# Linear attention on one core: half of the 17th head's output rows stored by GpSimd's queue

## The chip, the core and the metric

One NeuronCore of a Trainium2 chip runs one program on its five engines: TensorE (PE), VectorE (DVE), ScalarE (ACT), GpSimd (POOL) and SyncE (SP). Sixteen DMA engines move data between DRAM and the on-chip memory SBUF. The metric is the device time of one execution in microseconds (us), as a median over runs.

## The reference

Linear attention for 32 heads, each with 2048 rows of 128 bf16 elements in `q`, `k` and `v`:

```python
phi_q = jnp.where(q > 0, q + 1, jnp.exp(q)) + 1e-6
phi_k = jnp.where(k > 0, k + 1, jnp.exp(k)) + 1e-6
kv = jnp.einsum("bhsd,bhse->bhde", phi_k, v)
z = jnp.einsum("bhsd->bhd", phi_k)
num = jnp.einsum("bhqd,bhde->bhqe", phi_q, kv)
den = jnp.einsum("bhqd,bhd->bhq", phi_q, z)[..., None] + 1e-6
return num / den
```

Each head reads 1.5 MB and writes 0.5 MB: 50.33 MB read and 16.78 MB written in all.

## The kernel before

A head's 2048 rows lie in SBUF as 128 partitions of 16 rows each, so one partition is 16 x 128 bf16 = 4 KB, contiguous in DRAM. Each operation of head `h` has a key with a part number, such as `ldk16.0`, and the program runs each engine through a list of keys written out by hand (`ORDER`). An operation names the operations that it depends on, and the program turns these into semaphore waits.

For each head `h`:

- `ldq`, `ldk`, `ldv` (line 340) load 512 KB each, into rings of 7 buffers (`NI`).
- `ek` (ScalarE, line 366) and `em` (VectorE, 344) make min(exp(k), 1) + 1e-6; `rk` (GpSimd, 351; VectorE for the first heads) makes max(k, 0). The sum of the two is phi_k.
- `v1` (GpSimd, 376) copies `v` beside a column of ones, so that one product gives both kv and z.
- `kv` (TensorE, 383) sums 32 products of 128 x 129; `kvs` (VectorE, 355) takes the sum to SBUF.
- `T` (TensorE, 393) transposes `q`; `eq` (ScalarE, 397), `emq` (VectorE, 344), `rqa` (ScalarE, 349) and `rqb` (VectorE, 350) do for `q` what was done for `k`.
- `n` (TensorE, 415, 420, 422) makes numerator and denominator in two parts; `a` (435), `r` (438) and `f` (442), on VectorE, divide, and write the result into one of 16 output buffers (`NO`).
- `st` (line 450) stores the head's output, 512 KB, from SBUF to DRAM.

All loads but one (`ldv0.0`, on ScalarE's queue) and all stores are issued by SyncE, in the order of its list: loads first, and stores more and more towards the end, the 17th head's `st16.0` after `st17.0` and before `st14.0`. With 16 output buffers nothing waits for `st16.0` but the end of the program. After its last store SyncE waits for the semaphore of every output buffer (line 468).

A DMA of 128 partitions puts 8 partitions on each of the sixteen DMA engines, as descriptors of 4 KB. Two stores are cut by partitions: head 12 into 51, 64 and 13 (`ROWS`), and the first half of the columns of head 14 into 68 and 60 (`HALF`). `st_parts(h)` gives the parts of a head as columns a:b and partitions x:y.

GpSimd's list holds only `rk` and `v1` of the heads, and two operations of the start that make the identity matrix. In the middle of the kernel it reads `rk20.0 rk21.0 v121.0 rk22.0 v122.0 v123.0 rk23.0`. `rk22.0` waits for `kv20`, as there are two buffers for each of `rk` and `v1`.

Of the kernel before, what the change touches and what calls it, by code (L numbers as in the profile page):

```python
# [13 lines left out]
NI, NO, NE, NR, NV, NQ, NK = 7, 16, 2, 2, 2, 2, 2  # L14
# [31 lines left out]
def na(h):  # L46
    return NA[h] if h else 0


def groups(h):  # L50
    if h == NH - 1:
        return ((0, 2, 3, 0), (6, 2, 3, 2), (12, 2, 2, 4))
    return ((0, 4, 3, 0), (12, 2, 2, 4))


HALF = {14: ((0, 68), (68, 128))}
ROWS = {12: ((0, 51), (51, 115), (115, 128))}


def st_parts(h):  # L60
    tiles = ((0, 6), (6, 12), (12, 16)) if h == NH - 1 else WHOLE
    if h in HALF:
        tiles = HALVES
    return tuple((a, b, x, y) for i, (a, b) in enumerate(tiles)
                 for x, y in (HALF.get(h, ()) if i == 0 and h in HALF else ROWS.get(h, ((0, P),))))

# [20 lines left out]
def rqb_parts(h):  # L87
# [4 lines left out]
    if h == NH - 1:  # L92
# [48 lines left out]
    "POOL": """  # L141
        ident0 ident v10.0 rk4.0 v14.0 rk5.0 v15.0 rk6.0 v16.0 rk7.0 v17.0 v18.0 rk8.0 rk9.0 v19.0 rk10.0
        v110.0 v111.0 rk11.0 v112.0 rk12.0 v113.0 rk13.0 v114.0 rk14.0 v115.0 rk15.0 v116.0 rk16.0 rk17.0
        v117.0 rk18.0 v118.0 v119.0 rk19.0 v120.0 rk20.0 rk21.0 v121.0 rk22.0 v122.0 v123.0 rk23.0 v124.0
        rk24.0 rk25.0 v125.0 rk26.0 v126.0 rk27.0 v127.0 rk28.0 v128.0 rk29.0 v129.0 rk30.0 v130.0 rk31.0
        v131.0
    """,
# [25 lines left out]
class Program:  # L173
# [10 lines left out]
    def add(self, eng, key, fn, deps=(), dma=None, inc=True):  # L184
        assert key not in self.op, key
        self.op[key] = (eng, fn, tuple(deps), dma, inc)
# [71 lines left out]
def bass_standalone__linear_attn_elu__prompt_kernel(nc: bass.Bass, q: bass.AP, k: bass.AP, v: bass.AP, out: bass.AP):  # L258
    B, H, S, D = q.shape
    assert D == P and S == 16 * P and B * H == NH  # L260
    NT = S // P
# [5 lines left out]
    qf, kf, vf, of = (t.rearrange("b h s d -> (b h) s d") for t in (q, k, v, out))  # L267
    rows = lambda t, h: t[h].rearrange("(p j) d -> p j d", j=NT)

    with ExitStack() as es:  # L270
# [17 lines left out]
        o_sb = sb([P, NO, NT, D])  # L288
# [7 lines left out]
        pr = Program(sem)  # L296
        add = pr.add
# [59 lines left out]
        def head(h):  # L357
# [15 lines left out]
            for i, (a, b) in enumerate(v_parts(h)):  # L373
                key = f"v1{h}.{i}"
# [25 lines left out]
            n = na(h)  # L400
# [46 lines left out]
                                [[m, nb], [1, m], [0, D]]), op=ALU.mult)  # L447
                add("DVE", f"f{h}.{i}", g, [f"r{h}.{i}"] + freed(NO, h, ("st", st_parts)))
            for i, (a, b, x, y) in enumerate(st_parts(h)):
                add("SP", f"st{h}.{i}", lambda e, a=a, b=b, x=x, y=y: e.dma_start(  # L450
                    rows(of, h)[x:y, a:b], o_sb[x:y, h % NO, a:b]),
                    [f"f{h}.{j}" for j, (t0, nb, m, b0) in enumerate(groups(h)) if t0 < b and a < t0 + nb * m],
                    dma=f"o{h % NO}")

        for h in range(NH):
            head(h)
# [7 lines left out]
        for e, engine in (("POOL", nc.gpsimd), ("SP", nc.sync), ("ACT", nc.scalar), ("PE", nc.tensor), ("DVE", nc.vector)):  # L464
            pr.emit(e, engine)
        last = f"o{(NH - 1) % NO}"
        for name in [f"o{s}" for s in range(NO) if f"o{s}" in pr.count and f"o{s}" != last] + [last]:
            nc.sync.wait_ge(pr.get(name), pr.count[name])


# [26 lines left out]
```

## Time and profile before

| | |
|---|---|
| time, median of 3 runs | 169.11 us (169.07 to 169.39) |
| the profiled execution | 169.41 us, span 168.1 us |
| granted TensorE clock in it | 0.988 |
| mean DMA rate over the span | 402 GB/s |
| stores on SyncE's queue | 38, of which 29 of 512 KB |
| a 512 KB store, issue to landing | 14.0 us median |

Times of single operations count from the start of the span. The span is the time between the first and the last instruction of the program in the profile; the profiled execution's own time is 1.3 us longer. Matmuls are pipelined, so a busy TensorE is not one at its peak. The DMA table lists queues: q1 is SyncE's, q10 ScalarE's, and q8 and q14 fetch instructions. A DMA's landing is the time at which its semaphore is full. "Issue" is the time that the issuing engine's sequencer spends on it; the data moves later.

### The profile page before, as it was taken

Reading aid. Unit: us, or ns where it says so; the run is one execution under the profiler, and the core shown is the slowest. Engines: PE = TensorE matmul, PEld = TensorE weight load, DVE = VectorE, ACT = ScalarE, POOL = GpSimd, SP = SyncE. Lnnn points to the kernel's source line nnn. Section 1 sums busy time; section 2 is a strip of 40 time slices with the busy share of each in tenths; the row PEclk is TensorE's granted clock in tenths of the full one; section 3 lists DMA queues with packets and bytes.
Section 4 is the critical chain, followed back from the end, with each engine's and each line's share of the span. In section 5 each row is a group of like instructions: output and inputs, shape, how many; then the busy total and the mean of one; then the engine's idle time right before and its main releaser. Section 6 shows DMA issues by size and latency. Waiting matters only on the chain.

```text
span 168.1 us, 6169 instructions
## 1 busy us (share of the span) xinstructions
PE 155.7 (93%) x2709; PEld 150.8 (90%) x2709; DVE 155.8 (93%) x309; ACT 149.4 (89%) x101; POOL 84.4 (50%) x63
## 2 busy tenths in 40 slices
PE   3999999999999999999599999999999999999650
PEld 1689999999999999999589999999999999999640
DVE  0499999999999999999999999999999999999971
ACT  3799999999999999999669999999999999997600
POOL 1100355566666666546926667676555566670000
PEclk9999999999999999999999999999999999999995
DMA  5999999999999999999999999999999999999996
GB/s 212 409 420 414 401 407 411 401 409 406 407 409 403 408 411 417 407 406 416 406 421 414 418 412 408 421 412 416 414 415 416 414 417 411 415 415 414 375 406 243
DMA packets 18910, 67.51 MB, mean 402 GB/s; under 512 B 2115, under 2 KB 2499, under 8 KB 18883
## 3 DMA queue, kind: packets, MB, share of 16 engines
q1 hardware_dynamic: 18739, 66.59, 98.6%
q8 instruction: 21, 0.34, 0.8%
q10 hardware_dynamic: 144, 0.52, 0.8%
q14 instruction: 6, 0.05, 0.1%
HBM read 50.33 MB, written 16.78 MB: 399 GB/s over the span
## 4 chain that ended last, share of the span: by engine, by line
DVE 52%; PE 40%; DMA 2%; ACT 2%; issue 1%; SPq 0%
DVE la L442 24%; PE la L383 16%; DVE la L344 14%; PE la L420 9%; PE la L422 8%; PE la L393 7%; DVE la L350 7%; DVE la L438 3%; DMA la<-in_k_dram 2%; DVE la L355 2%; ACT la L397 1%; DVE la L376 1%; DVE la L435 1%; ACT la L366 1%; PE la L415 0%
## 5 line engine op out<-in xcount | busy, mean ns | idle before, releaser
L442 DVE TENSOR_TENSOR la<-la 128x1536 bf16<-128x1536 f32 (+2 forms) x65 | 78.0, 1200 | 0.6
L351 POOL TENSOR_SCALAR la<-la 128x2048 bf16<-128x2048 bf16 x28 | 54.1, 1935 | 38.2 <-PE la L383 38.2
L420 PE MATMUL la<-la 128*128 128x129 bf16 x512 | 67.0, 219 | 0.3 <-DVE la L355 0.3
L422 PE MATMUL la<-la 128*128 128x129 bf16 x512 | 67.0, 219 | 0.0
L397 ACT ACTIVATE la<-la 128x2048 bf16<-128x2048 bf16 (+2 forms) x35 | 60.3, 1729 | 5.9 <-PE la L422 2.9
L366 ACT ACTIVATE la<-la 128x2048 bf16<-128x2048 bf16 (+1 forms) x33 | 61.4, 1860 | 3.3 <-DMA la<-in_k_dram 3.2
L383 PE MATMUL la<-la 128*128 128x129 bf16 x1024 | 63.4, 220 | 0.0
L383 PEld LDWEIGHTS la<-la 128*128 128x128 bf16 x1024 | 59.4, 98 | 0.7 <-DVE la L355 0.5
L422 PEld LDWEIGHTS la<-la 128*128 128x128 bf16 x512 | 49.6, 97 | 0.0
L420 PEld LDWEIGHTS la<-la 128*128 128x128 bf16 x512 | 47.9, 97 | 0.5 <-DVE la L355 0.4
L344 DVE TENSOR_SCALAR la<-la 128x2048 bf16<-128x2048 bf16 (+2 forms) x68 | 44.9, 697 | 0.0
L376 POOL COPY la<-la 128x1024 int32<-128x1024 int32 (+1 forms) x29 | 30.7, 1058 | 26.9 <-PE la L383 16.6
L393 PE MATMUL la<-la 128*128 128x128 bf16 x512 | 35.6, 222 | 2.2 <-DMA la<-in_q_dram 1.1
L393 PEld LDWEIGHTS la<-la 128*128 128x128 bf16 x512 | 30.8, 99 | 3.5 <-DMA la<-in_q_dram 2.0
L349 ACT ACTIVATE la<-la 128x1024 bf16<-128x1024 bf16 (+2 forms) x31 | 33.1, 1067 | 0.0
L350 DVE TENSOR_SCALAR la<-la 128x1024 bf16<-128x1024 bf16 (+2 forms) x37 | 23.7, 646 | 5.7 <-DMA la<-in_k_dram 4.3
L415 PE MATMUL la<-la 128*128 128x3 bf16 (+1 forms) x128 | 21.6, 168 | 2.7 <-DVE la L442 1.7
L415 PEld LDWEIGHTS la<-la 128*128 128x128 bf16 x128 | 12.5, 98 | 3.2 <-DVE la L442 2.1
L438 DVE RECIPROCAL la<-la 128x12 f32<-128x12 f32 (+2 forms) x65 | 12.8, 199 | 1.4 <-PE la L422 0.8
L355 DVE CAST la<-la 128x129 bf16<-128x129 f32 x32 | 8.0, 251 | 0.0
L331 PE MATMUL la<-la 128*128 128x480 bf16 x21 | 6.3, 441 | 1.5 <-POOL la L316 1.5
L331 PEld LDWEIGHTS la<-la 128*128 128x128 bf16 x21 | 2.2, 114 | 3.5 <-POOL la L316 1.5
(15 smaller groups left out, 10.3 us busy)
## 6 DMA issues: line engine op xcount, KB each, us to landing
la<-in_q_dram SPq DMA_DIRECT2D x32, 512.0 KB, 14.8
la<-in_k_dram SPq DMA_DIRECT2D x32, 512.0 KB, 14.8
la<-in_v_dram SPq DMA_DIRECT2D x31, 512.0 KB, 14.5
out_dram<-la SPq DMA_DIRECT2D x29, 512.0 KB, 14.0
la<-in_v_dram ACTq DMA_DIRECT2D x1, 512.0 KB, 5.8
out_dram<-la SPq DMA_DIRECT2D x2, 256.0 KB
out_dram<-la SPq DMA_DIRECT2D x2, 192.0 KB, 3.1
out_dram<-la SPq DMA_DIRECT2D x1, 204.0 KB
```

The source lines that it names most:

```text
L344: add(on(key, "DVE"), key, lambda e: e.tensor_scalar(t, t, 1.0, EPS, op0=ALU.min, op1=ALU.add), deps)
L349: "ACT": lambda e: e.activation(dst, src, ACT.Relu),
L350: "DVE": lambda e: e.tensor_scalar(dst, src, 0.0, None, op0=ALU.max),
L351: "POOL": lambda e: e.tensor_scalar(dst, src, BIG, 0.0, op0=ALU.min, op1=ALU.max)}[eng], deps)
L366: add("ACT", f"ek{h}.{i}", lambda e, a=a, b=b: e.activation(em_sb[:, h % NE, a:b], k_sb[:, h % NI, a:b], ACT.Exp), over("ldk", h, ldk_part ...
L383: ins = e.matmul(kv_ps, lhsT=src[:, j], rhs=v1_sb[:, h % NV, j, 0:NC], start=(j + part == 0), stop=(j == NT - 1 and part == 1))
L393: ins = e.transpose(xT[:, j], q_sb[:, h % NI, j], ident[:])
L397: add("ACT", f"eq{h}.{i}", lambda e, a=a, b=b: e.activation(emq_sb[:, h % NQ, a:b], xT[:, a:b], ACT.Exp), over("T", h, t_parts, a, b) + fr ...
L415: e.matmul(_ap(o_ps[:, :], o + D, [[NC, m]]), lhsT=ones[:], rhs=epsr[:, 0:m], start=True, stop=False, skip_group_check=True)
L420: e.matmul(to, lhsT=emq_sb[:, h % NQ, t], rhs=kvs_sb[:, h % NK, 0:NC], start=late and c == 0, stop=False, skip_group_check=True)
L422: ins = e.matmul(to, lhsT=rq_sb[:, h % NQ, t], rhs=kvs_sb[:, h % NK, 0:NC], start=False, stop=True, skip_group_check=True)
L442: return e.tensor_tensor(out=_ap(o_sb[:, :, :, :], first(o_sb[:, h % NO, t0, 0:1]) - first(o_sb[:, :, :, :]), [[m * D, nb], [D, m], [1, D] ...
```

## The change

`st16` is cut into three parts by partitions: 0 to 63 stay with SyncE, at the same place of its list (`st16.0`). Partitions 64 to 95 (`st16.1`) and 96 to 127 (`st16.2`) are issued by GpSimd, `st16.1` between `v121.0` and `rk22.0`, `st16.2` between `v122.0` and `v123.0`. In DRAM the 32 partitions of a part lie one behind the other, 128 KB; for `st16.1` that destination is written as 2 runs of 64 KB, for `st16.2` as 4 runs of 32 KB. The source stays 32 partitions of 4 KB. Each part has its own semaphore (`p16.1`, `p16.2`), and SyncE waits for these two first in its closing waits.

```diff
-ROWS = {12: ((0, 51), (51, 115), (115, 128))}
+ROWS = {12: ((0, 51), (51, 115), (115, 128)), 16: ((0, 64), (64, 96), (96, 128))}
+BY_POOL = {"st16.1": 2, "st16.2": 4}
...
-        v117.0 rk18.0 v118.0 v119.0 rk19.0 v120.0 rk20.0 rk21.0 v121.0 rk22.0 v122.0 v123.0 rk23.0 v124.0
+        v117.0 rk18.0 v118.0 v119.0 rk19.0 v120.0 rk20.0 rk21.0 v121.0 st16.1 rk22.0 v122.0 st16.2 v123.0 rk23.0 v124.0
...
-                add("SP", f"st{h}.{i}", lambda e, a=a, b=b, x=x, y=y: e.dma_start(
-                    rows(of, h)[x:y, a:b], o_sb[x:y, h % NO, a:b]),
+                key = f"st{h}.{i}"
+                to = rows(of, h)[x:y, a:b]
+                if key in BY_POOL:
+                    to = of[h, NT * x:NT * y].rearrange("(g r) d -> g (r d)", g=BY_POOL[key])
+                add("POOL" if key in BY_POOL else "SP", key, lambda e, a=a, b=b, x=x, y=y, to=to: e.dma_start(
+                    to, o_sb[x:y, h % NO, a:b]),
...
-                    dma=f"o{h % NO}")
+                    dma=f"p{h}.{i}" if key in BY_POOL else f"o{h % NO}")
...
-        for name in [f"o{s}" for s in range(NO) if f"o{s}" in pr.count and f"o{s}" != last] + [last]:
+        for name in [n for n in pr.count if n[0] == "p"] + [f"o{s}" for s in range(NO) if f"o{s}" in pr.count and f"o{s}" != last] + [last]:
```

## The prediction, on record before the result

> **What bounds the kernel now.** I read the page first, then the stretches, the waits and chain of the end, and last the packets and completion events of single DMAs.
>
> ```profile
> PE 155.7 (93%) x2709; PEld 150.8 (90%) x2709; DVE 155.8 (93%) x309; ACT 149.4 (89%) x101; POOL 84.4 (50%) x63
> DMA  5999999999999999999999999999999999999996
> q1 hardware_dynamic: 18739, 66.59, 98.6%
> q8 instruction: 21, 0.34, 0.8%
> q14 instruction: 6, 0.05, 0.1%
> ```
>
> TensorE, VectorE and the 16 DMA engines are all full; GpSimd is half idle. So the question is which of them ends last. The table of stretches, and the waits of SyncE's queue after 150 us:
>
> ```profile
> core 0: us, PE busy (x) PEld busy (x) DVE busy (x) ACT busy (x) POOL busy (x), PEclk, DMA share, GB/s
> 140.00:150.00 10.00, 10.00 (x186) 10.00 (x184) 9.93 (x19) 9.91 (x7) 6.69 (x5) 1.00 1.03 415
> 156.00:160.00 4.00, 2.38 (x45) 2.20 (x42) 3.93 (x11) 2.85 (x3) 0.00 (x0) 1.00 0.93 373
> 164.00:168.10 4.10, 0.00 (x0) 0.00 (x0) 0.70 (x1) 0.00 (x0) 0.00 (x0) 0.53 0.63 240
> ```
> ```profile
> SPq L450 <- DVE la L344: 5.8, 1, 5.8
> SPq L468 <- DMA out_dram<-la: 2.4, 2, 1.3
> ```
> ```profile
> 163.74 0.96 DVE la L442
> ```
>
> The last line is the last piece of the chain: VectorE ends at 164.70 and the last store (st31.1) is issued at 164.72. The span ends at 168.10, after SyncE's waits at L468 for stores. So the last 3.4 us are stores only, and the DMA share there is 0.63: some engines are done and others not. The trace keeps sixteen completion events per full DMA, one for each engine. For st24.0 they run 156.62, 156.72, 156.96, then 159.60, 159.64, 159.72, 159.98, then nine from 160.59 to 161.78. Behind it stand st29, st19, st28, st30 (512 KB each) and st31 in three pieces. On the latest engine the queue never empties: st30.0 reaches it at 166.72, st31 takes 1.33 us more, 168.05, and the last event is at 168.06. The three earliest engines run dry and wait for issues. What a last store needs without a queue: st31.0, issued 163.64, has its first event at 165.36, 1.72 us; st31.1 so would be home near 164.72 + 1.7 + 0.2 for the spread = 166.6. The end is thus set by the latest DMA engine, 1.4 us behind compute, not by the sum of bytes. A change of who carries the rows counts fully there.
>
> Why they differ: a 16 KB instruction packet (21 on q8, 1.05 us each) sits on one engine at a time. After that at 16.46 one engine's event of ldk4.0 falls from 18.0 to 19.4, and it keeps the lag. SP's partial stores are already uneven the other way. st12.0 (51 rows) has three data events (88.85, 88.91, 90.08), st14.0 (68 half rows) four (152.47, 153.11, 153.72, 154.25). Followed from DMA to DMA, the three engines of st12.0 are among the four of st14.0, so SP's narrow stores begin with the same engines; and one of those three, call it x, is the one that ends last (154.25, 155.49 at st21.0, 161.78 at st24.0). At st16.0 the four stand at 151.12, 151.73, 152.34 and 152.89 (x): 1.77, 1.16 and 0.55 us ahead of x.
>
> **The price of a row.** A 4 KB packet has a median of 159 ns, and an engine steps 1.25 us from one 512 KB DMA (8 rows each) to the next: 0.157 us a row, the same for loads and stores.
>
> **The change, part by part.** st16.0 on SP keeps 64 of 128 rows: 4 instead of 8 rows for each engine, -4 x 0.157 = -0.63 us on all sixteen. st12.1, also 64 rows, shows that this is spread over sixteen (sixteen events). The 32 + 32 rows come back on GpSimd's queue. On SP, 51 rows used 3 engines, 13 used 13, 60 used 15 and 68 used 4: the largest divisor up to 16. With 2 and 4 runs on the DRAM side I take 2 and 4 engines: 16 rows each on two engines, 8 each on four. Net: two engines +12 rows, +1.88 us; four engines +4 rows, +0.63 us; the rest -0.63 us.
>
> Which engines, no row shows, as GpSimd issues no data DMA before. Bounds: at best the two and the four are all early ones and the end moves by -0.63 us; at worst both stores start with the same first engines as SP's narrow ones, 16 + 8 + 4 - 8 = +20 rows, +3.1 us. The nearest row is SP's own narrow store, which starts with x's group. If x is one of the two: +1.88 us. If x is in the group but only among the four: x moves +0.63, but the engine 0.55 us ahead of it, carrying 16 rows, ends at -0.55 + 1.88 = +1.33 us. Were the two instead among the other late engines (up to 161.48 at st24.0), the end would move about -0.3 + 1.88 = +1.6 us. I take +1.7 us, between 1.33 and 1.88.
>
> The Trainium skill, "DMA: Bandwidth & Descriptors", section "Why a DMA increments its semaphore by 16 and not by 1", says that a DMA uses as many engines as divide the slowest dimension on both sides, SyncE's on the lowest-numbered, GpSimd's on consecutive ones from a moving cursor. By it, with a cursor at zero, the sum is +1.33 or +1.88 us and not +3.1, as the second store does not fall on the first's engines; the trace agrees on SyncE's half (3, 13, 15, 4).
>
> GpSimd's side. st16.1 needs f16.0 and f16.1 (ended 98.12), long done when its turn comes behind v121.0:
>
> ```profile
> 102.97 1.03 POOL L376 COPY la<-la 128x1024 int32<-128x1024 int32 x1
> 105.67 1.96 POOL L351 TENSOR_SCALAR la<-la 128x2048 bf16<-128x2048 bf16 x1 [1.67 <-PE la L383]
> 107.57 1.03 POOL L376 COPY la<-la 128x1024 int32<-128x1024 int32 x1
> 110.26 1.11 POOL L376 COPY la<-la 128x1024 int32<-128x1024 int32 x1 [1.66 <-PE la L383]
> ```
>
> It falls into the 1.67 us that GpSimd waits for kv20, ahead of rk22.0; st16.2 into the 1.66 us behind v122.0, ahead of v123.0. Behind them queue rk22.0 and v122.0 (end 108.60) for kv22, which starts at 113.00, and v123.0 and rk23.0 (end 113.23) for kv23 at 117.62: 4.4 us spare each. What one issue costs GpSimd no row shows: SP's issues take 0.33 to 2.39 us, ScalarE's one 0.41. Even 2.39 leaves 0.7 us outside the wait and inside the 4.4: nothing. Without that cover, past some 6 us each, kv22 and all behind it would slip.
>
> Loads. From 104 us to st16.0's turn (its events began at 149.14) the two engines run 16 rows, 2.5 us, later, and SP's loads behind them too. Least room between the last event of a load and its first use after 104 us: 3.2 us (ldk24, ldq24 and ldv27), 3.4 for ldv31. 2.5 fits, so compute should keep its 164.70; the 24 rows of the worst case, 3.8 us, would not quite. SP's closing waits grow by two semaphores that are long full: about 0.07 us each at 165 us, ahead of the wait that ends at 168.06, so nothing.
>
> Sum: 0 on compute, +1.7 us on the last engine. The profiled execution took 169.41 us with a span of 168.10, 1.3 us outside it; the median of the three times is 169.11. Span 168.1 + 1.7 = 169.8; 169.11 + 1.7 = 170.8 us for the median.
>
> **Rivals.** *The rows fall on early engines.* Three engines have 5.2 us to spare at st24.0 and three more 2.1 to 2.2; if the two carry 16 rows there and the four are early or middling, x loses 4 rows: -0.63 us, 168.5 us. If the four include one of the late ones at 161.2 to 161.5, it gains 0.63 and the end stands between 0 and +0.35. For it: there is real idle time there, and x is one engine. Against it: the two must be neighbours out of six or seven of sixteen, and nothing but a start away from SP's first engines would bring them there. It decides at 1.9 us: an engine that stands less than that ahead of x ends later than x does now if it carries 12 rows more.
>
> *The split is even after all.* If GpSimd's stores spread 2 rows over each of the sixteen, every engine has its 8 again and only the order changes: 169.1 us. For it: the source has 32 rows, divisible by 16. Against it: the two-run destination, and the events of 51 and 68 rows. The Trainium skill's "DMA: Bandwidth & Descriptors", section "Rules for kernel authors", holds that spreading DMAs over SP, ACT and GpSimd saves issue time only, as all run on the same engines; by that it would be 169.1 too. The 5.2 us between first and last engine here is what speaks against it.
>
> *GpSimd's descriptor work holds up VectorE.* VectorE is busy 19.86 of 20 us from 100 to 120, so each microsecond lost there moves 164.70; but compute has 1.4 us before it reaches the DMA end. Alone it decides only past 1.4 us; 2 us of it would give 169.1 + 0.6 = 169.7 us.
>
> **How the numbers follow.** The heavy pair on late engines, 0.59, +1.3 to +1.9 us (170.4 to 171.0) and a tail to +3.1, and the stall of VectorE, 0.03: slower, 0.62. Rows on early engines, 0.25, 168.5 to 168.9: faster. Even split, or the pair early and one of the four late, 0.13: within 0.2%, 168.8 to 169.4, which is about what a measurement here can tell from no change. The range 168.5 to 171.2 takes in the faster case and the slower one, and leaves out the two stores on the same engines (172.2), less than 1 in 10, and a stall of compute on top.
>
> **What would show it.** Right: a GpSimd queue in the DMA table with 64 packets of 4 KB; some engines' events of st24.0 moving by +1.9 and +0.6 us and the others by -0.6; VectorE still ending near 164.7; SyncE's closing wait for stores longer than 2.4 us. Wrong: last events earlier by 0.6 (the pair was early), all unchanged (even split), VectorE's end later than 166 (a stall), or waits of kv22 on GpSimd.

## The result: 0.6% slower, and the times spread

| | before | after |
|---|---|---|
| median, same chip | 169.26 us (169.07 to 169.88, 18 runs) | 170.18 us (169.33 to 171.02, 18 runs) |
| the profiled execution | 169.41 us, span 168.1 us | 169.33 us, span 168.0 us |

The ratio is 1.0056, with a 95% interval of 1.0037 to 1.0074: 0.95 us (0.63 to 1.25). The times of before lie within 0.8 us, those of after are strewn over 1.7 us. The profiled execution of after is the earliest of its 18, no slower than before. It shows what the change did, but not the loss; the loss shows in late executions, those that took longer, which the experiments gave.

The page of after, the lines that answer to those of before:

```profile
PE 156.6 (93%) x2709; PEld 151.4 (90%) x2709; DVE 155.7 (93%) x309; ACT 149.4 (89%) x101; POOL 85.3 (51%) x65
DMA  5999999999999999999999999999999999999996
q1 hardware_dynamic: 18675, 66.33, 98.2%
q8 instruction: 21, 0.34, 0.8%
q0 software_dynamic: 96, 0.26, 0.4%
out_dram<-la POOLq DMA_DIRECT2D x2, 128.0 KB, 5.5
```

GpSimd has two instructions more. q0 is its queue: 64 packets of 4 KB for data and 32 small ones for the semaphores, sixteen for each DMA. SyncE's q1 has exactly 64 packets fewer. Landing took 5.5 us from the issue.

GpSimd's timeline in the middle of the kernel (start, length, instruction, in brackets the idle time before it):

```profile
103.97 0.66 POOL L455 DMA_DIRECT2D out_dram<-la  x1
105.71 1.94 POOL L352 TENSOR_SCALAR la<-la 128x2048 bf16<-128x2048 bf16 x1 [1.08 <-PE la L384]
107.60 1.03 POOL L377 COPY la<-la 128x1024 int32<-128x1024 int32 x1
108.58 0.54 POOL L455 DMA_DIRECT2D out_dram<-la  x1
110.29 1.10 POOL L377 COPY la<-la 128x1024 int32<-128x1024 int32 x1 [1.17 <-PE la L384]
```

An issue takes 0.66 and 0.54 us, and each lies inside the wait: the idle time of 1.67 us before has become 1.08 us, and rk22.0 starts at 105.71 us after 105.67. The rows themselves went out as follows: of the 32 packets of st16.1 all sixteen engines took two each, side by side, all started between 107.79 and 108.37 us, with sixteen completion events from 108.75 to 109.14; of st16.2 as well, from 112.46 to 113.06 us, with one engine late at 113.42 and 113.73. Two runs in DRAM or four made no difference: the split is even.

The table of stretches (length, busy time of each engine, granted clock, DMA share, GB/s), SyncE's closing wait, and the last line of the chain:

```profile
140.00:150.00 10.00, 10.00 (x185) 10.00 (x183) 9.93 (x19) 9.91 (x7) 6.69 (x6) 1.00 1.03 415
156.00:160.00 4.00, 2.41 (x45) 2.23 (x42) 3.93 (x11) 2.85 (x3) 0.00 (x0) 1.00 0.93 375
164.00:168.00 4.00, 0.00 (x0) 0.00 (x0) 1.00 (x2) 0.00 (x0) 0.00 (x0) 0.50 0.64 246
```
```profile
SPq L473 <- DMA out_dram<-la: 1.8, 2, 1.3
```
```profile
164.08 0.96 DVE la L443
```

Everything is as before: compute ends at 165.04 us (164.70 before; the granted clock from 160 to 165 us is 0.68 here and 0.92 there), the same tail of stores follows, and st24.0's last event is at 161.67 us after 161.78. No engine moved by +1.9, +0.6 or -0.6 us.

### The profile page after: what moved, and what is told of

Read it like the earlier page. It is cut to its first block, busy times and chain, and to the rows that moved or that the text cites. A ratio compares the mean times of both kernels' runs of the same rounds, so it can differ in the third digit from the quotient of the medians.

```text
span 168.0 us, 6172 instructions
## 1 busy us (share of the span) xinstructions
PE 156.6 (93%) x2709; PEld 151.4 (90%) x2709; DVE 155.7 (93%) x309; ACT 149.4 (89%) x101; POOL 85.3 (51%) x65
## 4 chain that ended last, share of the span: by engine, by line
DVE 49%; PE 46%; DMA 2%; issue 0%
DVE la L443 24%; PE la L384 17%; DVE la L345 13%; PE la L394 9%; PE la L421 9%; PE la L423 8%; DVE la L351 6%; DVE la L439 3%; PE la L332 3%; DMA la<-in_q_dram 2%; DVE la L356 2%; DVE la L436 1%; DVE la L377 1%; PE la L416 0%
## 5 line engine op out<-in xcount | busy, mean ns | idle before, releaser
L332 PE MATMUL la<-la 128*128 128x480 bf16 x21 | 6.8, 472 | 1.5 <-POOL la L317 1.5
```

## Experiments

A late execution differs by 1 us or more, so each kernel below is judged by its median and by how far its times lie apart; the kernel before, measured beside them, kept within 0.6 to 0.8 us.

**Which part of the change is it?** First the changed kernel again:

> The changed kernel once more, for a second trace and its spread. Its 18 runs lie between 169.3 and 171.0 us, those of before between 169.1 and 169.9, and the one trace (169.33) shows GpSimd's 64 packets started within 0.6 us of each other, 32 at a time, that is 2 on each of sixteen engines. Theory A (the rows fall on other engines from run to run): a run at 170.3 or more has a few engines whose events after 113 us are 1.3 to 1.9 us later than before, and packets of one store strung out over 2.5 us or more. Theory B (the split is always even and the time is lost elsewhere): GpSimd's packets again within 0.6 us, and what is late in a run over 170 is VectorE's end or the last engine by another cause (an instruction packet, a slower packet). Median 170.2 by both, spread over 1 us.

170.45 us (169.66 to 170.72) against 169.26, ratio 1.006 (1.004 to 1.0081). This time the profiled execution was a late one, 170.59 us. In it GpSimd's 32 packets of st16.1 again started within 0.6 us (108.26 to 108.79), with sixteen events, and VectorE ended at 165.12 us, as in after (165.04). So theory A falls: the split is even in a late execution too, and what is late is not compute. Then GpSimd is taken out, with the three parts on SyncE, late or early:

```diff
-BY_POOL = {"st16.1": 2, "st16.2": 4}
+BY_POOL = {}
...
-        st17.0 st16.0 st14.0
+        st17.0 st16.0 st16.1 st16.2 st14.0        # e2_sp_late
...
-        st5.0 st6.0 ldq27.0 ldq24.0 st10.0
+        st5.0 st6.0 ldq27.0 ldq24.0 st16.1 st16.2 st10.0        # e3_sp_early
```

> The same cut of st16 into 64, 32 and 32 rows, all three on SP's queue, one behind the other at st16.0's place; nothing on GpSimd's queue. 32 rows go 2 to an engine there. Theory A and theory B with the cause in GpSimd's queue: as before the change, 169.1 to 169.4, spread below 0.4 us. If the cut itself (48 more completion packets, two more issues) costs: 169.5 to 170.2.

> The same cut, both 32-row parts on SP's queue but issued near 104 us, behind ldq24.0, so that the rows move at about the time at which GpSimd's move them. Theory A, or a cause in GpSimd's queue: 169.1 to 169.4 with a spread below 0.4 us. If it is the earlier time of these rows (loads behind them 0.6 us later) that costs: 169.7 to 170.5 and a spread like the change's.

And GpSimd is kept, with a plain destination of 32 runs:

```diff
-BY_POOL = {"st16.1": 2, "st16.2": 4}
+BY_POOL = {"st16.1": 32, "st16.2": 32}
```

> The change with both parts on GpSimd's queue, but with the destination written as 32 runs of one row instead of 2 and 4. Theory A, where the number of runs picks the engines: an even split, 169.1 to 169.4, spread below 0.4 us. Theory B, where the split is even in both and GpSimd's queue is the cause: as the change, median 170.2 and a spread over 1 us.

| | median (range) | ratio to before (95%) |
|---|---|---|
| e2_sp_late | 170.47 (169.53 to 170.63) | 1.0054 (1.0034 to 1.0073) |
| e3_sp_early | 170.43 (169.48 to 171.01) | 1.0080 (1.0065 to 1.0095) |
| e4_pool_plain | 170.41 (169.54 to 171.02) | 1.0066 (1.0044 to 1.0089) |

All three lose about as much, and spread about as much, as the changed kernel. So neither GpSimd's queue, nor its place in time, nor the number of runs is the cause: theory A falls again with e4, and a cause in GpSimd's queue falls with e2 and e3. What the three share with the change is that head 16's store has become three DMAs. Only e2's last line, a cost of the cut itself, is left, and its 169.5 to 170.2 us was too low. (Its 48 more completion packets are 32 in the trace: q1 has 18771 packets after 18739.)

**An instruction more, a DMA more, a cut, or head 16?** Four kernels, each the kernel before with one thing added: p1 gives SyncE a few waits that are long satisfied and no DMA; p2 cuts head 16's store in two (64 and 64 rows) on SyncE, one DMA more; p3 leaves it whole and moves it to GpSimd's queue behind v121.0; p4 cuts the store of head 20 in place, and leaves head 16's alone.

```diff
+PADS = (("SP", 84), ("SP", 86))                          # p1_pad_sp: at these places of SyncE's list
...
+            if (eng, at) in PADS:
+                for n in range(4):
+                    engine.wait_ge(self.get(f"k{n}.0"), 16)
...
+16: ((0, 64), (64, 128))                                 # p2_cut2_sp, in ROWS; st16.1 behind st16.0
...
+BY_POOL = {"st16.0": 128}                                # p3_pool_whole, st16.0 behind v121.0
...
+20: ((0, 64), (64, 96), (96, 128))                       # p4_cut_head20, in ROWS; st20.1 st20.2 behind st20.0
```

> The kernel before, with a few waits more on SP's queue near 100 us, all for semaphores that are long full; no DMA is added, cut or moved. The four kernels with head 16's store in three parts all ran at 170.4 us with a spread over 1 us, on either queue, so GpSimd is not the cause. Theory L (any instruction more on a queue changes which engines get the instruction packets): 170.4, spread over 1 us. Theory N (the two DMAs more in all, 32 completion packets, change it): 169.2, spread as before (0.6). Theory R (it is the rows of head 16): 169.2.

> The kernel before with st16 in two parts of 64 rows, both on SP's queue at the old place: one DMA more in all. Theory L: 170.4 and wide. Theory N: wide, between 169.6 and 170.4. Theory R: wide, 170.4.

> The kernel before with st16 uncut, all 128 rows in one DMA on GpSimd's queue at the place of st16.1: as many DMAs as before. Theory N: 169.2 with the spread of before (0.6). Theory L (one instruction more on GpSimd's list, one less on SP's): 170.4 and wide. Theory R: wide, 170.4.

> The kernel before with the store of head 20 instead of head 16 in parts of 64, 32 and 32 rows, on SP's queue at its old place: two DMAs more, st16 untouched. Theory N and theory L: 170.4, spread over 1 us. Theory R: 169.2, spread 0.6.

| | median (range) | ratio to before (95%) |
|---|---|---|
| p1_pad_sp | 169.37 (169.25 to 169.89) | 1.0005 (0.9996 to 1.0013) |
| p2_cut2_sp | 169.87 (169.19 to 171.73) | 1.0043 (1.0021 to 1.0066) |
| p3_pool_whole | 169.26 (169.15 to 169.86) | 1.0002 (0.9993 to 1.0010) |
| p4_cut_head20 | 170.40 (169.89 to 171.03) | 1.0059 (1.0039 to 1.0079) |

A whole head on GpSimd's queue costs nothing. One more cut, of another head and without GpSimd, costs the same as the change. Theory L falls with p1 and p3, theory R with p4. Two readings were left: the number of DMAs in an execution (134 before; theory N), or the cutting itself (rival C).

**Count or cut?** t1 has 136 DMAs and no new cut, as its two extra DMAs are tiny loads on GpSimd's queue; t2 has the change's cut and 134 DMAs, as head 12's store is whole again; t3 cuts eight late stores; t4 keeps 134 DMAs and only moves rows onto the three first engines.

```diff
+            add("POOL", f"tiny{i}", lambda e, i=i: e.dma_start(          # t1_tiny
+                tiny_sb[:, i], rows(qf, 16)[32 * i:32 * i + 32, 0, 0:64]), [], dma=f"p16.{i}")
...
-ROWS = {12: ((0, 51), (51, 115), (115, 128)), 16: ((0, 64), (64, 96), (96, 128))}
+ROWS = {16: ((0, 64), (64, 96), (96, 128))}                              # t2_whole12, against after
...
+**{h: ((0, 64), (64, 96), (96, 128)) for h in (13, 16, 17, 18, 20, 21, 23, 26)}   # t3_cut8, in ROWS
...
-ROWS = {12: ((0, 51), (51, 115), (115, 128))}
+ROWS = {12: ((0, 69), (69, 117), (117, 128))}                            # t4_rows69
```

> The kernel before, with head 16's store whole on SyncE, and two tiny loads (32 rows of 128 bytes, into a buffer that nobody reads) on GpSimd's queue at the places of st16.1 and st16.2: 136 DMAs for each execution, no store cut. Theory N (the number of DMAs for each execution): as with the changed kernel, the times of single runs spread over 1 us or more and the median is 170.2 to 170.7, ratio 1.004 to 1.009, though 8 KB are all that moves. Rival C (a store cut into parts is what does it): tight at 169.3, ratio 0.999 to 1.001.

> The changed kernel, with its two GpSimd stores, but head 12's store whole at st12.0's place instead of 51, 64 and 13 rows: 134 DMAs again. By 0.157 us a row the three engines of st12.0 lose 14 rows (-2.2 us) and the others gain 2 or 3 (+0.3 to +0.5), so the latest others, 0.3 us ahead of x in the kernel before, become the last at about +0.1: 169.3 to 169.6. Theory N: tight at that level (spread of the runs 0.9 us or less). Rival C: spread over 1 us or more, median 170 or later. If packets of instructions now fall otherwise, the level can be up to 1.5 us off, and what tells then is the spread.

> The kernel before with eight late stores of SyncE (heads 13, 16, 17, 18, 20, 21, 23, 26) cut in place into 64, 32 and 32 rows: 16 DMAs more, 150. Theory N with a period of 4, 8 or 16 DMAs (what differs from one execution to the next comes round again): tight again, at 169.3 to 169.6. Theory N without such a period: times spread over 1 us or more, median 170.2 or later. Rival C (each cut costs something): later than with one cut, 171 or more.

> The kernel before with head 12's rows cut as 69, 48 and 11 instead of 51, 64 and 13: the same 134 DMAs, but the three first engines, x among them, carry 23 + 3 + 1 = 27 rows instead of 17 + 4 + 1 = 22. If x sets the end, and a row costs 0.157 us: 5 x 0.157 = +0.8 us, st24.0's last event near 162.6, time 170.0 to 170.2, tight. If compute or the sum of bytes sets the end: 169.3, no change.

| | median (range) | ratio to before (95%) |
|---|---|---|
| t1_tiny | 169.47 (169.05 to 169.78) | 1.0001 (0.9990 to 1.0011) |
| t2_whole12 | 169.81 (169.56 to 170.27) | 1.0024 (1.0014 to 1.0035) |
| t3_cut8 | 172.99 (172.65 to 173.77) | 1.0218 (1.0195 to 1.0240) |
| t4_rows69 | 170.14 (169.90 to 170.23) | 1.0038 (1.0023 to 1.0053) |

Theory N falls with t1: two DMAs more, and neither the median nor the spread moves. C stands, and t3 bears it out: eight cuts cost 3.6 us. t2 fits neither as written. It is 0.4 us later, with a spread of 0.7 us; by C it should have spread as after does. Its level was mis-sized: head 12's parts of 64 and 13 rows put 4 or 5 rows on each of the other engines, so that a whole store gives them 3 or 4 more, not 2 or 3: +0.5 to +0.6 us. The latest of them, 0.3 us ahead of x, is then last by 0.2 to 0.3 us; st24.0's last event is at 161.95 us, +0.17. That it does not spread fits the reading that its three first engines carry 14 rows less and so have room for a delay, but that is argued from one trace and not shown. t4 belongs to the prediction's other step, and is taken up below. VectorE's last piece in its trace, which stood at 163.74 us in before, is this:

```profile
164.54 0.96 DVE L442 TENSOR_TENSOR la<-la 128x768 bf16<-128x768 f32 x1
```

**What a cut does.** The place to look is the stretch from 150 to 155 us, in which all DMA work but one packet of instructions is stores. Its row in the table of stretches, first of t1_tiny, then of p4_cut_head20 (a late execution, span 169.5 us), then of t3_cut8; the last two columns are the DMA share and GB/s:

```profile
150.00:155.00 5.00, 5.00 (x95) 4.97 (x92) 4.70 (x12) 2.98 (x4) 0.00 (x0) 1.00 1.03 415
```
```profile
150.00:155.00 5.00, 5.00 (x94) 4.97 (x92) 4.96 (x13) 2.97 (x3) 0.00 (x0) 1.00 1.02 397
```
```profile
150.00:155.00 5.00, 5.00 (x93) 4.97 (x91) 4.63 (x11) 4.18 (x4) 0.35 (x1) 1.00 0.79 246
```

In p4 the engines are as busy as in t1 and move less: single packets take longer. The trace's packets show it directly. A 4 KB packet takes 159 ns and a 2 KB one 84; the table counts, between 150 and 155 us, packets of 4 KB over 225 ns and of 2 KB over 150 ns (the one of 432 to 441 ns that starts where a packet of instructions ends, in every kernel, is left out). Beside it stands what SyncE spent on issuing st25.0 and st24.0, at about 148 to 154 us, and the last event of st14.0, the narrow store.

| kernel | late store cut | GB/s, 150 to 155 us | long packets | issues of st25.0 + st24.0 | st14.0's last event | span |
|---|---|---|---|---|---|---|
| before | no | 412 | 1 | 2.54 us | 154.25 | 168.1 |
| p1_pad_sp | no | 413 | 1 | 2.35 | 154.22 | 168.1 |
| p3_pool_whole | no | 415 | 1 | 2.19 | 153.91 | 167.8 |
| t1_tiny | no | 415 | 1 | 2.00 | 154.15 | 168.0 |
| after | yes | 409 | 6 | 3.88 | 153.81 | 168.0 |
| e2_sp_late | yes | 406 | 7 | 3.77 | 154.16 | 168.1 |
| e3_sp_early | yes | 399 | 13 | 3.38 | 154.35 | 168.2 |
| p2_cut2_sp | yes | 402 | 9 | 3.70 | 154.16 | 168.3 |
| e1_again | yes | 407 | 10 | 4.26 | 155.46 | 169.3 |
| e4_pool_plain | yes | 401 | 13 | 4.04 | 155.38 | 169.2 |
| p4_cut_head20 | yes | 397 | 15 | 3.07 | 155.69 | 169.5 |

The columns in the middle part the kernels without an overlap: 412 GB/s or more without a late cut, 409 or less with one; one long packet against six or more; 2.54 us against 3.07 or more. t4 (no cut) has 413 GB/s, 1 packet and 2.28 us, t2 (a cut) 408, 6 and 3.32. In t3 there are 76 long packets in these five microseconds.

The last two columns say when it costs time. Long packets alone do not: e3 has 13 and ends at 168.2 us, but eleven of them are 4 KB packets. In the three late executions the 2 KB packets of the narrow store are hit: what those over 104 ns took beyond 84 ns sums to 0.76, 1.35 and 1.88 us (e1, e4, p4), against 0 in before and 0 to 0.51 in the four with a cut that ended early. (t2 has 0.90; but there the engines of st14.0 carry less, st14.0 is done at 153.93 us, and other engines end last.) st14.0 sits on the four engines of which one, the prediction's x, ends last. There its last event falls 1.1 to 1.4 us later, and the end follows it: from that event to the end of the span it is 13.8 to 13.9 us in before and in these three. How much of the delay the 2 KB packets make is not shown, as the trace names no engine for a packet; in e1 their 0.76 us are less than its 1.2. Compute has no part in it. The last piece of p4's chain, against after's 164.08 us:

```profile
162.56 0.96 DVE la L442
```

VectorE ends 1.5 us earlier in p4 than in after, and the execution ends 1.5 us later. (The early end is not the cut's doing: in p3, without one, VectorE ends at 163.51 us too.) SyncE's waits for its last stores grow instead, from 1.8 us in after:

```profile
SPq L468 <- DMA out_dram<-la: 3.8, 3, 1.4
```

t3 shows a second loss behind the first. These are SyncE's waits from 133 us to the end, first before, then t3_cut8:

```profile
SPq L450 <- DVE la L344: 5.8, 1, 5.8
SPq L450 <- DVE la L355: 4.3, 2, 3.3
...
SPq L450 <- DVE la L438: 2.4, 1, 2.4
SPq L450 <- DVE la L442: 1.2, 2, 1.0
```
```profile
SPq L468 <- DMA out_dram<-la: 1.3, 1, 1.3
SPq L450 <- DVE la L438: 1.0, 1, 1.0
```

Before, SyncE spends 13.7 us of the tail waiting for VectorE's results, so its issues are early. In t3 one wait of 1.0 us is left: it issues back to back, its last store is issued at 168.84 us though VectorE ended at 164.82, and the page shows the engines slowed and short of work from the 35th slice on:

```profile
DMA  5999999999999999999999999999999999978998
GB/s 205 412 415 413 406 407 407 406 409 405 408 410 405 407 418 410 415 396 416 415 414 420 414 416 411 411 418 416 419 415 411 419 409 411 367 247 257 346 407 334
```

SyncE's room for issues in the tail is thus not large; but a single cut does not use it up. In p4, with two issues more, 8.5 us of waits for VectorE are left.

**What stays open.** Why packets of other stores take 150 to 490 ns once a full store is cut late, and why SyncE's issues get longer in the same microseconds, no run tells. Both begin while the cut store's rows move: at 148.4 us in p4, whose cut store is three places earlier in the list, and at 150.9 to 151.3 us in after, e3 and e4, whose long packets start there. Cuts of early stores, where loads still share the engines, were not tried on their own; head 12's two late parts, which land between 130 and 143 us in before, leave little: from 135 to 140 us every kernel has one to four long packets, and t2, where that store is whole, has one.

## Why the prediction was right in sign and range, and wrong in its reason

- **The end is set by the latest DMA engine, not by compute: right.** t4 tests it by itself: the three first engines carry 23 + 3 + 1 = 27 rows instead of 22. At 0.157 us a row that is +0.79 us. st24.0's last event went from 161.78 to 162.51 us (+0.73), the last landing from 168.06 to 168.84 (+0.78); the ratio gives +0.64 us (0.39 to 0.90). The three are x's group, as the prediction traced it from DMA to DMA: three of st14.0's four events move by 0.8 us, and the fourth stays. Compute could be taken for the cause, as VectorE ended 0.8 us later too in that execution (165.50 after 164.70). But by the prediction's 1.7 + 0.2 us for a last store without a queue, the store issued at 165.52 would have been home near 167.4, not 168.84. And in p3 and t1, VectorE ended at 163.51 and 164.05 us with spans of 167.8 and 168.0: compute that ends earlier gains next to nothing.
- **"With 2 and 4 runs on the DRAM side I take 2 and 4 engines": this step failed.** The split is two rows on each of sixteen engines, with 2 and 4 runs as with 32 (e4: 64 packets again, sixteen events each). Nothing moved by +1.88, +0.63 or -0.63 us, and the whole term of +1.7 us with it is void. SyncE's narrow stores were the wrong neighbour: their counts of 51, 13, 60 and 68 rows don't divide by sixteen, those of the change do; in e2 the 32-row parts have sixteen events each on SyncE's queue too. By the rule that the prediction took from the Trainium skill, "DMA: Bandwidth & Descriptors", section "Why a DMA increments its semaphore by 16 and not by 1", two and four engines would have carried the rows. The same section of the Trainium skill names an exception on trn2 that the prediction left out: some direct copies from GpSimd use all sixteen engines, with the partitions divided by 16, rounded up, on each. For 32 partitions that is two on each, and the trace agrees (64 packets, sixteen events for each store).
- **The rival "the split is even after all" had the mechanism, at 169.1 us, and not the time.** Its price for the rest, nothing, was wrong: it left out that a full store becomes three DMAs. p3 is that rival without the cut, and it stands at 169.26 us, ratio 1.0002. The Trainium skill, on the same page, section "Rules for kernel authors", says that spreading DMAs over the queues saves issue time only; this run of the whole store agrees.
- **The cost that decided was in no step.** "st12.1, also 64 rows, shows that this is spread over sixteen" was true of where the rows go, and was taken to settle what a cut costs. The cut costs 0.95 us (0.63 to 1.25), 0.73 us (0.36 to 1.12) as two parts in p2, unevenly from one execution to the next. That 170.18 us (+0.95) lies near the forecast of 170.8 (+1.7) is therefore luck: two different losses of like size.
- **GpSimd's issues hidden, compute untouched: right.** 0.66 and 0.54 us against waits of 1.67 and 1.66 us; VectorE's pieces from f13.1 to f30.1 end within 0.04 us of before; only the last two, f31.0 and f31.1, are 0.34 us later. The rival of a stall of VectorE has nothing for it.
- **"What would show it" was half met.** GpSimd's 64 packets are there, and VectorE ended near 164.7 (165.04); but SyncE's closing wait was 1.8 us and not longer than 2.4, and the events of st24.0 said "all unchanged (even split)", and it was this line, not the median, that told the reason was wrong.

## What to carry to other kernels

Where a kernel's end is set by its most loaded DMA engine, rows on that engine can be priced from the trace and moved for a known sum (five rows, 0.6 to 0.8 us), but a cut is not free: one full store cut late cost 0.7 to 1.4 us on the median, though every engine carried as many rows as before. Look at the spread of the times before trusting one profile: the profile of after was its best execution and showed no loss at all. And a forecast that meets the time should still be held against the events it named: here not one engine moved as it said.

## What the runs showed of the hardware

- A DMA of GpSimd with 32 rows of 4 KB used all sixteen engines, two rows each, whether its destination was written as 2, 4 or 32 runs.
- From the end of GpSimd's issue to the first packet passed 3.2 to 3.3 us with 4 KB packets (st16.1: 104.63 to 107.79), and with 128 rows 3.2 us as well (p3: 103.11 to 106.27). The issue itself took 0.54 to 0.70 us, for 32 rows of 128 bytes, 32 of 4 KB and 128 of 4 KB alike.
- Two tiny DMAs, 8 KB in all with 32 semaphore packets of 9 ns, cost nothing in the time (1.0001, 0.9990 to 1.0011), while a cut that added as many DMAs cost 0.95 us.
- Full DMA share does not mean full rate: 1.02 of share moved 397 GB/s in one kernel, and 1.03 moved 415 in another.
